# Loading the second channel weight of a token-and-channel mixer in whole rows, and reordering it in ScalarE's scaling passes

## The chip, the cores and the metric

The kernel runs on one core of a Trainium2 chip. The metric is the time of one launch on the device in microseconds (us); the median of several runs is given, with the lowest and the highest. Beside these runs there is one execution under the hardware profiler, which has a time of its own.

## What is computed

The reference is an attention block without softmax, followed by an MLP mixer, in float32:

```
kv  = einsum('bhsd,bhse->bhde', k, v)
a   = einsum('bhsd,bhde->bhse', q, kv)
a   = a / sqrt(mean(a*a, -1) + 1e-6) * g_norm
x   = a as (batch, seq, heads*dim)
u   = x + (relu(x^T @ w_tok1) @ w_tok2)^T
out = u + relu(u @ w_ch1) @ w_ch2
```

There are 8 batches with 8 heads, 576 rows and a head width of 64, so x has 512 columns. w_tok1 is 576 x 256, w_tok2 256 x 576, w_ch1 512 x 1536 and w_ch2 1536 x 512. The four weights come as 64-bit floats. The kernel has to turn them into 32-bit floats itself; everything else is 32-bit.

## The kernel before

**Stages.** The core first computes attention and token mixing, two batches at a time (four pairs). Then it does channel mixing over the rows of u, five groups in all; the first group is smaller and has code of its own (`channel1_once`, `channel2_once`), and the others run through `channel1` and `channel2`. The channel products use two nested levels of a fast 2 x 2 block scheme with seven products in place of eight. The blocks, their sums and differences are made by VectorE, ScalarE and GpSimd beside the matmuls.

**Order of the work.** Every instruction is held in the order of the program on its engine. That order is written out by hand for attention and token mixing, as strings of step names (`start`, `middle`, `steady`, `last`) that `play` carries out one by one. Nearly all transfers are issued on SP's queue by the helper `dma` (L121), in program order; a store that adds to what is in memory goes through GpSimd.

**Decoding a weight.** A weight is fetched in blocks. A block's raw words lie in a staging tile `raw` of 1024 pairs (low word, high word) in each partition, of which there are four. `decode` (L159) has four steps. `scale` runs on ScalarE: a pass over the high words writes the destination as a scaled float (L163), and a pass over the low words scales these in place (L166). The other three run on VectorE: `clamp` (L169), `shift` (L173) and `add` (L178), a custom instruction that adds the top of the low word to the result. `stream` (L1238) strings the blocks together so that a block is scaled before its predecessor's `add`. A digit in the hand-written order stands for so many further steps of this stream. The names f0 to f13 in the order stand for the fetches of the 14 channel blocks; f8 to f13 are the six blocks of w_ch2, 256 rows each.

**The order of leaves.** Channel mixing needs the columns of w_ch2 in an order that fits 32 x 32 transposes on VectorE. A row of 512 columns is read as (h, b, l, j), where h is the half (2), b a block (4), l a leaf (2) and j a column (32), and is stored in each half as (l, b, j). Before the change the transfers do this: `get_ch2` (L222) gives one transfer for each pair of row group, leaf and half, so eight in a block, each of runs of 32 columns, that is 256 bytes.

**The tile and its other uses.** `w_ch2` (L105) is one tile of 4 quarters x 6 row groups x 256 columns in each partition. A block fills two row groups in each of two quarters. Before its rows are filled, part of the tile is used for something else: `turn_early` (L640, steps x00 to x21) parks transposed blocks of u in row groups 2 to 5 of a quarter, and `put_blocks` (L624, steps b00 to b21) stores them to memory, from where `fetch_once` and `fetch_u` read them back. The order of parking is: quarters 2, 3, 0 and 1, and later 2 and 3 again. Later `mix_ch2` (L265) forms the outer sums from the quarters, `originals` and `split` (L291, L297) store the parts for the later groups, and `w2_of` (L277) gives a quarter or a sum to the first group's matmuls.

Of the kernel before, what the change touches and what calls it, by code (L numbers as in the profile page):

```python
# [11 lines left out]
F32 = mybir.dt.float32  # L12
U32 = mybir.dt.uint32
U16 = mybir.dt.uint16
AF = mybir.ActivationFunctionType
# [5 lines left out]
def kernel(  # L21
# [32 lines left out]
    nc = tc.nc  # L54
    P = 128
    B, S, DM = k.shape
# [7 lines left out]
    NC, NF, NTOK = DM // P, DCH // P, DTOK // P  # L64
    HP = H // 2
    DH = DM // 2
# [3 lines left out]
    NS = NF // 2  # L70
# [7 lines left out]
    def pool(name, bufs, side="left", stack=ctx, **kw):  # L78
        return stack.enter_context(tc.tile_pool(name=name, bufs=bufs, side=side,
                                                reuse_waits="tile", **kw))  # L80

    w1s, w2s = ExitStack(), ExitStack()
    w1p, w2p = pool("w1", 1, "left", w1s), pool("w2", 1, "right", w2s)
# [18 lines left out]
    w_tok2 = tokw.tile([P, NTOK, S], F32, name="w_tok2")  # L102

    w_ch1 = w1p.tile([P, 4, 4, FQ], F32, name="w_ch1")
    w_ch2 = w2p.tile([P, 4, NS, DH], F32, name="w_ch2")  # L105
    k_in = [inp.tile([P, JJ, DH], F32, name=f"k_in{i}") for i in range(4)]
    v_in = [inp.tile([P, JJ, DH], F32, name=f"v_in{i}") for i in range(4)]
    kvp = [inp.tile([P, HP, P], F32, name=f"kvp{i}") for i in range(2)]
    u_rest = dram.tile([J * P, DM], F32, name="u_rest")
    u_rows = lambda u: u_rest if u == B else out[u, :LO]  # L110

    def do(f, *a, **kw):
        return lambda: f(*a, **kw)

    late = {}


    keep = tc.keep_in_program_order

    def dma(o, i, engine=nc.sync):  # L120
        keep(engine.dma_start(o, i))  # L121
# [34 lines left out]
            q_rest[b] = qtp.tile([P, HP, HF], F32, name="qR", tag="qR", bufs=4)  # L156
            dma(q_rest[b], q[b].rearrange("(c p) s -> p c s", p=P)[..., LO:])

    def decode(dst, raw, flat):  # L159

        bits = dst.bitcast(U32)
        def scale():
            keep(nc.scalar.activation(dst, raw()[..., 1].bitcast(F32), AF.Prelu,  # L163
                                      scale=2.0 ** -112, alpha=2.0 ** 32))
            low = raw()[..., 0]
            keep(nc.scalar.activation(low, low, AF.Copy, scale=2.0 ** -29))  # L166

        def clamp():
            keep(nc.vector.tensor_scalar(out=dst, in0=dst, scalar1=TOP, scalar2=-TOP * 2.0 ** 32,  # L169
                                         op0=ALU.min, op1=ALU.max))  # L170

        def shift():
            keep(nc.vector.tensor_scalar(out=bits, in0=bits, scalar1=3, scalar2=None,  # L173
                                         op0=ALU.logical_shift_left))

        def add():
            o = bits.bitcast(U16)
            keep(nc.vector._custom_dve(ADD32_U16LIMBS, out=o, in0=o, in1=flat().bitcast(U16)[..., :2]))  # L178

        return scale, clamp, shift, add  # L180

    def words(w):
        return w.bitcast(U32).rearrange("r (n w) -> r n w", w=2)
# [2 lines left out]

        return flat if len(dst.shape) == 2 else flat.rearrange("p (a n) -> p a n", a=dst.shape[1])

    def block(n, loads, dst):

        raw = []

        def fetch():
            raw.append(stage.tile([P, n, 2], U32, name="raw", tag="raw", bufs=4))
            for o, i in loads(raw[0]):
                dma(o, i)

        def turn():
            t = raw[0]
            return t if len(dst.shape) == 2 else t.rearrange("p (a n) w -> p a n w", a=dst.shape[1])  # L200

        return (fetch,) + decode(dst, turn, lambda: raw[0])

    def get_tok1(t):

        rows = words(moe_w_tok1)[:LO].rearrange("(j p) n w -> p j n w", p=P)
        return block(J * P, lambda raw: [(raw.rearrange("p (j n) w -> p j n w", j=J),
                                          rows[:, :, ts(t, P)])], w_tok1[:, :J, ts(t, P)])

    def get_tok1_rem():  # L210
        w = words(moe_w_tok1)[LO:]
        return block(DTOK, lambda raw: [(raw[:HF], w), (raw[HF:], w)], w_tok1[:, J])

    def get_tok2(t):
        return block(S, lambda raw: [(raw, words(moe_w_tok2)[ts(t, P)])], w_tok2[:, t])
# [5 lines left out]

    def get_ch2(f):  # L222

        a = 2 * (2 * f // NS)

        def loads(raw):
            t = raw.rearrange("p (h f l b j) w -> p f l h b (j w)", h=2, f=2, l=2, b=NC)
            rows = words(moe_w_ch2)[ts(f, 2 * P)].rearrange("(f p) (h b l j) w -> f l p h b (j w)", f=2, h=2, b=NC, l=2)
            return [(t[:, i, l, h], rows[i, l, :, h]) for i in range(2) for l in range(2) for h in range(2)]

        dst = w_ch2[:, a:a + 2, ds(2 * f % NS, 2)]
        return block(2 * DM, loads, dst.rearrange("p h f n -> p h (f n)"))

# [29 lines left out]
    def mix_ch2():  # L265


        firsts, lasts = [], []
        for i in range(2):
            t1, t2, t4 = (late["d2"][:, n, ts(i, NS // 2)] for n in range(3))  # L270
            b11, b12, b21, b22 = (w_ch2[:, n, ts(i, NS // 2)] for n in range(4))
            sub = lambda o, a, b: do(tensor_add, o, a, b, ALU.subtract)
            firsts += [sub(t1, b12, b11), sub(t2, b22, t1)]
            lasts += [sub(b12, b12, b22), sub(t4, b21, t2)]
        return firsts, lasts

    def w2_of(n):  # L277
        i = {1: 0, 7: 1, 2: 2, 3: 3}
        return w_ch2[:, i[n]] if n in i else late["d2"][:, {5: 0, 6: 1, 4: 2}[n]]

    parts_dram = {(w, o): dram.tile([P, 7, FQ], F32, name=f"parts{w}{o}")
                  for w in (1, 2) for o in SA}
# [3 lines left out]
    def part_of(weight, o, n):  # L286
        if weight == 1:
            return (w_ch1[:, SA[o]] if SA[o] < 4 else late["w2"][:, SA[o] - 4])[:, SA[n]]
        return w2_of(o)[:, ts(int(n in (2, 3)), W), ts(int(n in (7, 3)), P)]
# [328 lines left out]
    def turn_tile(y, x, i):  # L618
        for o in range(2):
            keep(nc.vector.transpose(  # L620
                y[:, :, o, 2 * i:2 * i + 2].rearrange("p b n t -> p n b t"),
                x[:, ts(o, DH)].rearrange("p (n b t) -> p n b t", n=2, b=NC)))
# [16 lines left out]

    def turn_early(u, half):  # L640
        pair, c = u // 2, 2 * (u % 2) + half
        y = w_ch2[:, (c + 2) % 4 if pair == 0 else 2 + c, 2:].rearrange("p b (o n t) -> p b o n t", o=2, n=NC)
        for i in range(2):
            turn_tile(y, X[pair, c][:, i], i)
        blocks[u, half] = y
# [154 lines left out]
    def channel2_once(g):  # L800
# [11 lines left out]
        def product(n, ps, start, stop):  # L812
            for p in range(2):
                for s in range(NS):
                    matmul(ps[:, p], lhsT=late["once"][n - 1][:, s, p], rhs=w2_of(n)[:, s],
                           start=(start and p == 0 and s == 0), stop=stop,
                           skip_group_check=True)
# [122 lines left out]
    def sub(t, i, j):  # L940

        return t[:, ts(i, W), j]
# [308 lines left out]
    def play(lines, after={}, **stages):  # L1251
# [3 lines left out]
        for name in " ".join(lines).split():  # L1255
# [5 lines left out]
            else:  # L1261
# [5 lines left out]
    tok2 = [get_tok2(t) for t in range(NTOK)]  # L1267
    channel = ([get_ch1(c, f) for f in range(2) for c in range(NC)]
               + [get_ch2(f) for f in range(NF // 2)])
    load(0)  # L1270
    for block in tok1[:2]:
# [20 lines left out]
    for block in tok1[2:] + tok2:  # L1292
# [35 lines left out]
    more = {f"w{n}{k}": f for n, b in enumerate(tok1 + tok2) for k, f in enumerate(b)}  # L1328
    more |= {f"f{n}": b[0] for n, b in enumerate(channel)}
    more |= {f"x{u}{half}": do(turn_early, u, half) for u in range(3) for half in range(2)}  # L1330
    more |= {f"b{u}{half}": lambda u=u, half=half: put_blocks(u, half, blocks[u, half])
             for u in range(3) for half in range(2)}
# [46 lines left out]

    fetch_x(0)  # L1380
    firsts, lasts = mix_ch2()
    parts2 = [f for o in ORDER2 for f in split(2, o)]

# [79 lines left out]
```

## Time and profile before

| | us |
|---|---|
| median of 3 runs | 781.64 |
| lowest, highest | 778.35, 783.63 |
| profiled execution, time | 777.2 |
| profiled execution, span from first to last instruction | 775.4 |
| TensorE (PE) busy | 761.0 |
| VectorE (DVE) busy | 643.2 |
| ScalarE (ACT) busy | 277.4 |
| GpSimd (POOL) busy | 112.4 |

PEld is the weight load of TensorE, SP the engine that issues most transfers, and a name with q at its end (SPq) the queue of that engine. A row of instructions in order of time gives the start, the time taken, the engine, the line in the kernel, the operation, what is written and read, the shape and the count; the idle time of the engine before it and what ended this stand in brackets. A row of waits gives who waited for whom, then the total in us, the count and the longest. A row of transfers gives what is written and read, the issuing queue, the count, the size of each and the median time from issue to landing. Line numbers are those of the kernel before; a helper's line stands for all its callers, so tiles tell such rows apart: `raw` is the staging tile, `w_ch` is either channel weight, `ps_...` are banks of PSUM.

### The profile page before, as it was taken

The page shows a single profiled execution, that of the slowest core. Times are in us where ns is not written, and L with a number is a line of the kernel's source. Part 1 is how long each engine was busy: PE and PEld are TensorE (multiplying, and loading weights), DVE is VectorE, ACT ScalarE, POOL GpSimd, SP SyncE. Part 2 cuts the span into 40 slices and gives each one's busy share as a digit, 9 for nine tenths or more (in the row PEclk, how much of TensorE's full clock was granted, in tenths as well). Part 3 has the DMA queues.
Part 4 walks back from the last instruction along what each step waited for, and adds up shares of the span by engine and source line. Part 5 has one row for each costly group of instructions (what it writes and reads, how often), then busy time and mean ns, then how long its engine had stood idle before and what let it go on. Part 6 is the DMA issues. An engine that isn't in the chain of part 4 may idle for free.

```text
span 775.4 us, 12776 instructions
## 1 busy us (share of the span) xinstructions
PE 761.0 (98%) x4682; PEld 611.6 (79%) x4682; DVE 643.2 (83%) x946; ACT 277.4 (36%) x549; POOL 112.4 (14%) x128
## 2 busy tenths in 40 slices
PE   5999999999999999999999999999999999999997
PEld 5655555545888888888888888888888888888887
DVE  2867887897776868989978889987998996798996
ACT  2566575665210233521134242223352223325220
POOL 1002021113410000002240001042000218000204
PEclk9999999999999999999999999999999999999999
DMA  9999999999899696599998577999659879855679
GB/s 293 322 330 375 370 354 281 253 259 362 281 279 358 256 301 189 166 274 184 233 230 262 148 216 224 256 188 268 199 147 285 174 218 207 207 147 159 150 192 117
DMA packets 177820, 188.30 MB, mean 243 GB/s; under 512 B 74464, under 2 KB 140512, under 8 KB 177760
## 3 DMA queue, kind: packets, MB, share of 16 engines
q1 hardware_dynamic: 140752, 167.55, 71.5%
q0 software_dynamic: 34816, 18.36, 16.1%
q10 hardware_dynamic: 2192, 1.61, 0.7%
q8 instruction: 37, 0.61, 0.3%
q14 instruction: 23, 0.19, 0.1%
HBM read 138.31 MB, written 49.15 MB: 242 GB/s over the span
## 4 chain that ended last, share of the span: by engine, by line
PE 94%; DVE 3%; DMA 1%; ACT 1%; issue 1%; SPq 0%; DVEq 0%; ACTq 0%
PE ps_d L133 27%; PE ps_b L133 19%; PE ps_a L133 18%; PE ps_u L133 8%; PE ps_h L133 8%; PE ps_v L133 5%; PE ps_c L133 3%; PE ps_o L133 2%; PE ps_kv L133 2%; PE ps_w L133 2%; DMA raw<-in_moe_w_tok_dram 1%; ACT x L499 1%; DVE r L124 0%; DVE sv L124 0%; DVE x L445 0%
## 5 line engine op out<-in xcount | busy, mean ns | idle before, releaser
L133 PE MATMUL ps_d<-ui,w 128*128 128x256 f32 x504 | 118.6, 379 | 0.0
L133 PEld LDWEIGHTS ps_d<-ui,w 128*128 128x128 f32 x504 | 95.8, 190 | 13.0
L130 ACT COPY ps_d<-ps_a 128x768 f32<-128x768 f32 (+1 forms) x56 | 32.0, 572 | 202.1 <-PE ps_a L133 199.1
L124 DVE TENSOR_TENSOR v<-v,v 128x1536 f32<-128x1536 f32 (+2 forms) x70 | 103.2, 1482 | 0.3
L133 PE MATMUL ps_b<-sv,w 128*128 128x256 f32 x324 | 79.2, 380 | 0.1
L133 PE MATMUL ps_a<-v,w 128*128 128x256 f32 x324 | 78.8, 379 | 0.0
L1200 POOL DMA_DIRECT2D out_dram<-us x24 | 26.8, 1831 | 292.6 <-ACT p L130 287.3
L133 PEld LDWEIGHTS ps_b<-sv,w 128*128 128x128 f32 x324 | 60.8, 190 | 10.2 <-issue 2.1
L133 PEld LDWEIGHTS ps_a<-v,w 128*128 128x128 f32 x324 | 61.6, 190 | 8.4
L133 PE MATMUL ps_h<-x,w_tok 128*128 128x512 f32 (+1 forms) x160 | 65.4, 603 | 0.5 <-DVE x L503 0.4
L133 PE MATMUL ps_u<-h,w_tok 128*128 128x512 f32 (+1 forms) x160 | 64.7, 599 | 0.0
L133 PE MATMUL ps_d<-v,w 128*128 128x256 f32 x258 | 62.7, 379 | 0.0
L127 ACT ACTIVATE v<-v 128x768 f32<-128x768 f32 (+1 forms) x54 | 42.6, 821 | 55.1 <-DVE v L124 55.1
L1200 POOL DMA_DIRECT2D out_dram<-r x40 | 41.3, 1923 | 103.2 <-ACT p L130 80.3
L133 PE MATMUL ps_d<-sv,w 128*128 128x256 f32 x228 | 55.4, 379 | 0.0
L133 PEld LDWEIGHTS ps_d<-v,w 128*128 128x128 f32 x258 | 48.9, 190 | 6.6
L133 PEld LDWEIGHTS ps_h<-x,w_tok 128*128 128x128 f32 (+1 forms) x160 | 26.2, 189 | 32.3 <-issue 27.3
L133 PEld LDWEIGHTS ps_u<-h,w_tok 128*128 128x128 f32 (+1 forms) x160 | 25.6, 179 | 31.1 <-issue 26.7
L133 PEld LDWEIGHTS ps_d<-sv,w 128*128 128x128 f32 x228 | 43.3, 190 | 5.9
L133 PE MATMUL ps_a<-uT,w 128*128 128x256 f32 x192 | 46.7, 379 | 0.0
L133 PE MATMUL ps_b<-ui,w 128*128 128x256 f32 x168 | 40.8, 379 | 0.0
L133 PEld LDWEIGHTS ps_a<-uT,w 128*128 128x128 f32 x192 | 36.5, 190 | 5.0
(162 smaller groups left out, 1278.0 us busy)
## 6 DMA issues: line engine op xcount, KB each, us to landing
w<-parts SPq DMA_DIRECT2D x168, 384.0 KB, 3.7
w<-parts SPq DMA_DIRECT2D x56, 192.0 KB, 3.8
uT<-blocks SPq DMA_DIRECT2D x36, 256.0 KB, 5.3
k_in<-in_k_dram SPq DMA_DIRECT2D x16, 512.0 KB, 8.7
qT<-in_q_dram SPq DMA_DIRECT2D x8, 1024.0 KB, 9.5
out_dram<-x POOLq DMA_DIRECT2D x16, 512.0 KB, 6.4
v_in<-in_v_dram SPq DMA_DIRECT2D x14, 512.0 KB, 9.0
raw<-in_moe_w_ch_dram SPq DMA_DIRECT2D x8, 768.0 KB, 7.7
```

Source lines behind the costliest of these rows:

```text
L124: keep(engine.tensor_tensor(out=o, in0=a, in1=b, op=op))
L127: keep(nc.scalar.activation(o, a, AF.Relu))
L130: keep(nc.scalar.copy(o, a))
L133: keep(nc.tensor.matmul(*a, **kw))
L499: keep(nc.scalar.activation(x[:, k, h], x[:, k, h], AF.Copy, scale=inv[:, k, h]))
L1200: keep(nc.gpsimd.dma_start(to, t()[ds(b * Q, Q), at].rearrange("p n l j -> p n (l j)"), accum_op=ALU.add))
```

## The change

`get_ch2` now makes two transfers for a block, one for each row group, of whole rows: 512 columns of 8 bytes, 4 KB in a piece. The staging tile thus holds the columns in the order of memory. The order of leaves is made by ScalarE: `scale_leaves` runs in place of `scale` for these six blocks and has four passes, two over the high words (one for each leaf) and two over the low words. The low words are written over the high words that have been used, and `add` reads them there.

The tile is laid out anew, as 2 pairs of quarters x 6 row groups x 2 quarters x 256 columns, so that a block is one run of 1024 columns. `w2_quarter(n)` gives a quarter in the new layout, with rows of 256 at a step of 512; the users of the tile go through it.

```diff
-    w_ch2 = w2p.tile([P, 4, NS, DH], F32, name="w_ch2")
+    w_ch2 = w2p.tile([P, 2, NS, 2, DH], F32, name="w_ch2")
+    w2_quarter = lambda n: w_ch2[:, n // 2, :, n % 2]
...
+        def scale_leaves():
+            of = raw().rearrange("p (g b l j) w -> p g l b j w", g=4, b=NC, l=2)
+            to = lambda t, l: t.rearrange("p (g l b j) -> p g l b j", g=4, l=2, b=NC)[:, :, l]
+            for l in range(2):
+                keep(nc.scalar.activation(to(dst, l), of[:, :, l, ..., 1].bitcast(F32), AF.Prelu,
+                                          scale=2.0 ** -112, alpha=2.0 ** 32))
+            for l in range(2):
+                keep(nc.scalar.activation(to(raw()[..., 1], l), of[:, :, l, ..., 0], AF.Copy, scale=2.0 ** -29))
...
-            keep(nc.vector._custom_dve(ADD32_U16LIMBS, out=o, in0=o, in1=flat().bitcast(U16)[..., :2]))
-        return scale, clamp, shift, add
+            keep(nc.vector._custom_dve(ADD32_U16LIMBS, out=o, in0=o, in1=flat().bitcast(U16)[..., 2 * leaves:][..., :2]))
+        return scale_leaves if leaves else scale, clamp, shift, add
...
     def get_ch2(f):
-        a = 2 * (2 * f // NS)
         def loads(raw):
-            t = raw.rearrange("p (h f l b j) w -> p f l h b (j w)", h=2, f=2, l=2, b=NC)
-            rows = words(moe_w_ch2)[ts(f, 2 * P)].rearrange("(f p) (h b l j) w -> f l p h b (j w)", f=2, h=2, b=NC, l=2)
-            return [(t[:, i, l, h], rows[i, l, :, h]) for i in range(2) for l in range(2) for h in range(2)]
-        dst = w_ch2[:, a:a + 2, ds(2 * f % NS, 2)]
-        return block(2 * DM, loads, dst.rearrange("p h f n -> p h (f n)"))
+            t = raw.rearrange("p (f n) w -> p f n w", f=2)
+            rows = words(moe_w_ch2)[ts(f, 2 * P)].rearrange("(f p) n w -> f p n w", f=2)
+            return [(t[:, i], rows[i]) for i in range(2)]
+        dst = w_ch2[:, 2 * f // NS, ds(2 * f % NS, 2)]
+        return block(2 * DM, loads, dst.rearrange("p f h n -> p (f h n)"), True)
...
-            b11, b12, b21, b22 = (w_ch2[:, n, ts(i, NS // 2)] for n in range(4))
+            b11, b12, b21, b22 = (w2_quarter(n)[:, ts(i, NS // 2)] for n in range(4))
...
-        return w_ch2[:, i[n]] if n in i else late["d2"][:, {5: 0, 6: 1, 4: 2}[n]]
+        return w2_quarter(i[n]) if n in i else late["d2"][:, {5: 0, 6: 1, 4: 2}[n]]
...
-        y = w_ch2[:, (c + 2) % 4 if pair == 0 else 2 + c, 2:].rearrange("p b (o n t) -> p b o n t", o=2, n=NC)
+        y = w2_quarter((c + 2) % 4 if pair == 0 else 2 + c)[:, 2:].rearrange("p b (o n t) -> p b o n t", o=2, n=NC)
```

More of the change, by code (lines that the diff above doesn't have):

```diff
@@ L157, in load_q_rest, with decode @@
             dma(q_rest[b], q[b].rearrange("(c p) s -> p c s", p=P)[..., LO:])
-    def decode(dst, raw, flat):
+    def decode(dst, raw, flat, leaves=False):
         bits = dst.bitcast(U32)
@@ L187, in like, with block @@
         return flat if len(dst.shape) == 2 else flat.rearrange("p (a n) -> p a n", a=dst.shape[1])
-    def block(n, loads, dst):
+    def block(n, loads, dst, leaves=False):
         raw = []
@@ L200, in turn @@
             return t if len(dst.shape) == 2 else t.rearrange("p (a n) w -> p a n w", a=dst.shape[1])
-        return (fetch,) + decode(dst, turn, lambda: raw[0])
+        return (fetch,) + decode(dst, turn, lambda: raw[0], leaves)
     def get_tok1(t):
```

## The prediction

> **What bounds the kernel now.** I read the page's table of busy times first, to see which engine fills the span, and then busy times by stage, cut where the changed loads begin (about 117 us) and where the last block of this weight is rounded (about 190 us).
>
> ```profile
> span 775.4 us, 12776 instructions
> PE 761.0 (98%) x4682; PEld 611.6 (79%) x4682; DVE 643.2 (83%) x946; ACT 277.4 (36%) x549; POOL 112.4 (14%) x128
> ```
>
> ```profile
> 0.00:20.00 20.00, 11.82 (x144) 11.31 (x144) 5.42 (x13) 4.31 (x7) 2.77 (x14) 1.00 0.94 292
> ...
> 117.00:131.00 14.00, 14.00 (x104) 6.66 (x95) 13.36 (x30) 6.43 (x16) 1.68 (x3) 1.00 0.96 290
> 131.00:149.00 18.00, 17.41 (x273) 9.88 (x272) 10.76 (x22) 11.61 (x27) 0.74 (x1) 1.00 1.05 257
> 149.00:172.00 23.00, 23.00 (x123) 9.99 (x123) 21.97 (x35) 14.93 (x30) 5.25 (x7) 1.00 0.95 255
> 172.00:190.00 18.00, 18.00 (x52) 7.79 (x49) 15.66 (x21) 11.78 (x20) 4.19 (x6) 1.00 1.04 344
> ```
>
> After the two bounds of a stage come its length and the busy times of TensorE, its weight loads, VectorE, ScalarE and GpSimd, then clock, DMA share and GB/s. TensorE works for 761.0 of 775.4 us. Of the 14.4 us without work, 8.2 lie in the first 20 us, before this weight is touched. In the four stages that the change touches TensorE is idle for 18.00 - 17.41 = 0.59 us in all, while the DMA engines are full (0.95 to 1.05). A busy matmul row need not be at its peak, so I looked at the chain that ended last: from 157.14 to 188.78 us it is matmuls alone (40 of ps_h in 15.85 us, 40 of ps_u in 15.80), 439 ns for a pass over 512 columns as in the stages around. Full DMA engines therefore hold nothing up here. The one wait of TensorE between 50 and 190 us is this:
>
> ```profile
> PE ps_o L133 <- ACT x L499: 0.6, 1, 0.6
> ```
>
> It ends with attention's scaling of x at 143.7 us, when of the six blocks only the first had been scaled (130.81) and none rounded (from 149.26).
>
> **What the skill says.** "DMA: Bandwidth & Descriptors", section "Specifications", puts the smallest transfer at line rate at 512 B; pieces are now 256 B and become 4 KB. The trace agrees in direction: between 146 and 150 us, nearly all 256 B, the queue's 2158 packets carried 0.53 MB for 67.7% of 16 engines, 20 ns each; between 102 and 112 us, pieces of 1 KB and more, 2.87 MB cost 84.5%, 47 us of one engine per MB against 82. "ScalarE: Activation LUTs", section "What ACT_TABLE_LOAD costs", prices an activation with immediate operands at 186 ns + 0.833 ns per element, less 93 ns where two follow each other: 1.04 us for 1024 elements, 0.61 for 512. The trace's passes over the raw words, which step over every other word, take 1.16 us, a tenth longer. "SBUF — State Buffer", section "SBUF: two separate sides", says that transfers and engines use different ports; so lighter transfers should not quicken TensorE. No run yet tests that.
>
> **Part 1, the loads.** Six blocks of 1 MB go from 8 transfers of 128 KB (4096 pieces of 256 B) to 2 of 512 KB (256 pieces of 4 KB).
>
> ```profile
> raw<-in_moe_w_ch_dram SPq DMA_DIRECT2D x8, 768.0 KB, 7.7
> raw<-in_moe_w_ch_dram SPq DMA_DIRECT2D x48, 128.0 KB, 4.4
> ```
>
> The columns are count, size and the time from issue to landing; the first row is the other channel weight, whose pieces of 6 KB are the nearest thing to the new load. 36 issues go, 36 x 0.54 us (the median of this issue) = 19 us of SP's queue. DMA time falls from 24,576 pieces x 20 ns / 16 = 31 us of all engines to 6.3 MB x 47 / 16 = 18.5 us. A block is whole sooner: now from the first issue (118.65 us for the first block) to the scaling pass at 130.81, some 12 us; then about 8, by the 768 KB row. Everything behind on SP moves forward: q and k rows, the stored turned blocks, the fetch of uT at 171.86. On the path that sets the end: nothing, since TensorE waits for none of them (uT is first multiplied at 188.72). **0 us.** Should the cover go, and TensorE be faster here by 13 us, this would be worth its 12.5 us; nothing in this change does that.
>
> **Part 2, the scaling passes.** Each block has two passes of 1024 (L163, L166) and gets four of 512, two high and two low. Measured: the two start 1.06 us apart and the second ends 1.16 later, 2.2 us. Four of 512, by the copies of that width (0.60 us, three in 1.64): 3 x 0.52 + 0.60 = 2.2 us; the skill's price gives two passes 1.99 and four 2.17. So +0 to +0.2 us a block, at most 1.1 us of ScalarE for six. The unknown is the shape: sources of 16 runs of 32 words in place of one run. From below, it costs nothing (the passes already step by 8 bytes). From above, I let each double, +2.2 us a block. I take +0.2. The block that counts is the last:
>
> ```profile
> 177.09 1.17 ACT L163 ACTIVATE w_ch<-raw 128x1024 f32<-128x1024 f32 x1 [0.99 <-DVE w_ch L178]
> 178.16 1.14 ACT L166 ACTIVATE raw<-raw 128x1024 uint32<-128x1024 uint32 x1
> 179.21 0.56 ACT L130 COPY x<-ps_u 128x512 f32<-128x512 f32 x1
> 179.67 0.59 ACT L130 COPY ps_u<-x 128x512 f32<-128x512 f32 x1
> ```
>
> Behind the passes stands the copy that seeds tile 5 (done at 180.26). TensorE comes to it after 20 matmuls of 439 ns from 172.99, at 181.77: 1.5 us of slack. +0.2 is hidden; +2.2 would stop TensorE for 0.7 us. Each of the other blocks has idle time of ScalarE next to it (0.5 to 2.6 us). **0 us.**
>
> **Part 3, the waits.** The pass at 177.09 waited 0.99 us for the addition of an earlier block (L178), that at 155.75 1.54 us likewise (the addition ran from 153.64 to 155.72). Those blocks write other rows, but their two separate halves span one another. In the new layout a block is one run of 1024, so I expect both waits to go, 2.5 us of ScalarE idle time. Late next is the landing, and behind that TensorE, which is not waiting. The passes also wait for two transfers each in place of eight. **0 us** on the path.
>
> **Part 4, the layout.** Quarters now lie in pairs, rows of 256 at a step of 512. The three rounding steps on VectorE keep 1024 elements (0.68, 0.68, 1.22 us); the addition reads the word beside the one it read. The sums (L124, 768 elements in 0.95 us), the 24 transposes (0.40 each), matmul operands of 256 and stores in pieces of 1 KB keep counts and sizes. **0 us**, with 0.1 us on either side for a transpose or a sum whose rows step further.
>
> **Sum.** 0 us, bounds -0.6 (the whole wait of TensorE in the stage) and +0.7. The profiled execution took 777.2 us, so 777 again; the median, 781.64 of three (778.35 to 783.63), lies 4.4 above it, and the profile can't show where. I take 0.6 off, since runs of longer time may hold a late transfer in the full stage: **781.0 us**.
>
> **The rivals.** *False waits between quarters (slower).* Turned blocks are parked in this tile. If their writes are ordered by span rather than by row, the second half's transposes must wait for the store of the first, its neighbour in the new layout:
>
> ```profile
> 83.47 1.42 DVE L620 STREAM_TRANSPOSE w_ch<-x 128x256 f32<-128x256 f32 x4
> 84.81 0.92 DVE L178 CUSTOM_DVE_ANT_1 w_ch<-w_ch,raw 128x1536 uint16<-128x1536 uint16 x1
> 85.64 1.28 DVE L445 TENSOR_TENSOR x<-ps_o,g_sb 128x512 f32<-128x512 f32 x2
> ...
> 86.17 3.47 SPq L121 DMA_DIRECT2D blocks<-w_ch  x4
> ```
>
> The store is issued from 86.17 to 89.64 and lands 2.9 us later (the row for these stores), so VectorE would stand from 83.5 to 92.5, 9 us. Queued behind it: an addition, attention's gains at 85.64 and its sums. The k-v products at 93.66 need the banks that those gains free at 86.92; 9 us later is 95.9, a stop of 2.3 us; VectorE then has 3.6 idle us to 104 and 0.6 to 117 to catch up, and what is left stops TensorE later. Some 5 to 9 us, 7 taken: **788.6**. It decides from 6.7 us of delay on (93.66 - 86.92). For it: the two waits of part 3 look like order by span. Against: a pass of the other weight began at 127.41 while the shift of the rows interleaved with it ran only at 128.53; only additions have shown the loose order.
>
> *Relief that the profile can't show (faster).* If the 4.4 us between profile and median are late transfers in the full stage, 12.5 us less DMA time could win most: **777.5**. Against: the profiled execution has just as full engines and no such wait.
>
> *Passes at twice the time:* +0.7 on ScalarE's path, **782.3**, and more only if several seeds are late.
>
> **How the numbers follow.** No change, 0.78; false waits, 0.12; relief, 0.06; slow passes, 0.04. About 1% is what a measurement of this kernel can tell from no change. The range reaches from the relief, with a little for the spread, to the middle of the false waits: 777.0 to 787.0. Faster by over 1% (below 773.8) would need more than half of all idle time of TensorE, mostly from stages not touched: 0.03. Slower by over 1% (above 789.5) is the dear half of the false waits and what I haven't thought of: 0.09. Within 1%: 0.88.
>
> **What would show it.** Right: 12 loads of 512 KB landing in 5 to 9 us, DMA share well below 0.95 between 131 and 172 us, 24 passes of about 0.6 us, no wait of L163 for L178, TensorE idle for 0.6 us or less from 50 to 190. Wrong: transposes (L620) that wait for a store of blocks; passes over 0.8 us; TensorE waiting for a seed near 182 us.

## The result and the profile after

The changed kernel takes 776.97 us, the median of 20 runs (776.47 to 778.63). The kernel before, run beside it, takes 778.32 (777.42 to 783.63, 20 runs). The ratio is 0.9974 with a 95% interval of 0.9963 to 0.9985: faster by about 2.0 us, which is also the difference of the means (779.10 and 777.09). The medians differ by 1.35 us, because much of the gain is a tail that is gone: 7 of the 20 runs before took over 779 us, and none of those after. The profiled execution took 776.47 us (777.2 before).

The head of its profile, and busy times by stage, with the columns as in the prediction:

```profile
span 774.6 us, 12729 instructions
PE 760.8 (98%) x4682; PEld 611.6 (79%) x4682; DVE 642.7 (83%) x946; ACT 279.4 (36%) x561; POOL 112.4 (15%) x128
```

```profile
117.00:131.00 14.00, 14.00 (x98) 6.72 (x95) 13.36 (x30) 8.17 (x19) 1.67 (x3) 1.00 1.00 347
131.00:149.00 18.00, 18.00 (x274) 10.03 (x274) 11.39 (x23) 10.76 (x28) 1.16 (x2) 1.00 0.73 260
149.00:172.00 23.00, 23.00 (x123) 9.90 (x121) 22.30 (x35) 16.04 (x38) 4.83 (x7) 1.00 0.81 259
172.00:190.00 18.00, 18.00 (x51) 8.29 (x50) 14.35 (x20) 11.50 (x22) 4.92 (x7) 1.00 1.03 367
```

TensorE's work is what it was (761.0 and 760.8 us). In the stage from 131 to 149 us, 17.41 busy us became 18.00: the only wait of TensorE between 50 and 190 us has gone, and the waits of the kernel after list none there. The DMA share between 131 and 172 us fell from 1.05 and 0.95 to 0.73 and 0.81. So 0.6 us of the gain can be read directly, and it is the very wait that the prediction put down to ScalarE. What ended it is seen when SP's issues are set beside TensorE. The kernel before, in order of time (`qT` is the tile of q rows that attention multiplies next):

```profile
117.36 11.12 SPq L121 DMA_DIRECT2D raw<-in_moe_w_ch_dram  x9
128.53 3.93 SPq L121 DMA_DIRECT2D blocks<-w_ch  x8
132.57 4.38 SPq L121 DMA_DIRECT2D raw<-in_moe_w_ch_dram  x8
137.05 1.54 SPq L121 DMA_DIRECT2D qT<-in_q_dram  x1
...
141.66 2.02 ACT L499 ACTIVATE x<-x,inv 128x64 f32<-128x64 f32 x8 [1.92 <-issue]
143.77 1.16 PE L133 MATMUL ps_o<-kvp,qT 64*64 64x64 f32 x64 [0.59 <-ACT x L499]
```

The kernel after, in order of time:

```profile
117.56 2.15 SPq L122 DMA_DIRECT2D raw<-in_moe_w_ch_dram  x3
119.77 9.38 SPq L122 DMA_DIRECT2D blocks<-w_ch  x8
129.37 0.84 SPq L122 DMA_DIRECT2D raw<-in_moe_w_ch_dram  x2
130.31 0.38 SPq L122 DMA_DIRECT2D qT<-in_q_dram  x1
...
141.58 2.02 ACT L507 ACTIVATE x<-x,inv 128x64 f32<-128x64 f32 x8 [1.91 <-issue]
143.03 1.16 PE L134 MATMUL ps_o<-kvp,qT 64*64 64x64 f32 x64
```

The scaling of x runs until 143.60 us in the kernel after, yet TensorE starts its matmuls at 143.03. They do not need the end of that scaling, so the label on the wait before was wrong. What they need is `qT`. The instructions on this tile, first of the kernel before, then of the kernel after:

```profile
L121 SPq DMA_DIRECT2D qT<-in_q_dram x1: 1542/1542/1542, 137.0 to 137.0; - x1
...
DMA to landing us min/median/max: 6.6/6.6/6.6
```

```profile
L122 SPq DMA_DIRECT2D qT<-in_q_dram x1: 378/378/378, 130.3 to 130.3; - x1
...
DMA to landing us min/median/max: 6.9/6.9/6.9
```

Before, the q rows are issued at 137.05 and land 6.6 us later, at 143.65; TensorE starts 0.12 us after that. After, they are issued at 130.31 and land at 137.2, 5.8 us early. The time from issue to landing hardly differs; the place in the queue does. Ahead of the q rows on SP stand one fetch of w_ch2 (f8), eight stores of turned blocks, and another fetch (f9), 8 + 8 + 8 issues before and 2 + 8 + 2 after (the first row of each view also holds one load of the other weight). From the start of that first row to the issue of the q rows SP needs 19.7 us before and 12.8 us after.

### The profile page after: what moved, and what is told of

It reads as the page before. It is cut to its first block, busy times and chain, and to the rows that moved or that the text cites. A ratio compares the mean times of both kernels' runs of the same rounds, so it can differ in the third digit from the quotient of the medians.

```text
span 774.6 us, 12729 instructions
## 1 busy us (share of the span) xinstructions
PE 760.8 (98%) x4682; PEld 611.6 (79%) x4682; DVE 642.7 (83%) x946; ACT 279.4 (36%) x561; POOL 112.4 (15%) x128
## 3 DMA queue, kind: packets, MB, share of 16 engines
q1 hardware_dynamic: 117136, 167.54, 70.2%
## 4 chain that ended last, share of the span: by engine, by line
PE 93%; DMA 5%; DVE 2%; issue 0%; ACTq 0%; SPq 0%; DVEq 0%
PE ps_d L134 27%; PE ps_b L134 19%; PE ps_a L134 18%; PE ps_u L134 8%; PE ps_h L134 7%; PE ps_v L134 5%; PE ps_c L134 3%; DMA v_in<-in_v_dram 2%; PE ps_w L134 2%; PE ps_kv L134 2%; PE ps_o L134 2%; DMA qR<-in_q_dram 1%; DMA k_in<-in_k_dram 1%; DVE r L125 0%; DVE sv L125 0%; DVE xg L125 0%
```

## The experiments

Three theories. **Q**: the q rows (fetched by the step `lq1`) stood behind the fetches and were late, by 0.6 us in the profile and by more in some runs. **L**: less DMA work in this stretch helps in general, by whatever transfer. **W**: the gain comes from the waits that went, the passes or the layout. Each run is compared with runs of the kernel before on the same chip.

**Q rows ahead of the second fetch, nothing else.** The kernel before with one step moved in the hand-written order; loads of 256 bytes, passes and layout stay.

```diff
-        "kv00 kv01 e00 e01 -d40 f9", "-u8 -a3 -q30 -g31 -q31 -g30 -t30 -t31 -m3 -r3 -lq1",
+        "kv00 kv01 e00 e01 -d40", "-u8 -a3 -q30 -g31 -q31 -g30 -t30 -t31 -m3 -r3 -lq1 f9",
```

> The kernel before with one step moved: the transfer of the q rows for the second half of a pair (-lq1, 1 MB) stands ahead of the fetch f9 on SP's queue, not behind it. Theory Q (TensorE's wait at 143 us is for these rows, which queue behind 24 small transfers): the rows are issued at about 132.6 us in place of 137.05, land near 139, TensorE's only wait between 50 and 190 us (0.59 us) goes, and the timed ratio to the kernel before is that of the changed kernel, 0.9963 to 0.9985. Theory L (the gain is less DMA work in the full stage, whichever transfers): nothing changes there, ratio 0.9995 to 1.0005. Theory W (the gain is from waits of ScalarE and VectorE that the new layout drops): ratio 1.000 as well.

It took 777.52 us (776.25 to 780.13, 22 runs), with 779.17 (777.10 to 784.67, 52 runs) for the kernel before; ratio 0.9969, interval 0.9956 to 0.9982. Over 779 us were 2 of 22 runs, against 30 of 52. Its profile in order of time:

```profile
130.03 3.90 SPq L121 DMA_DIRECT2D blocks<-w_ch  x7
134.03 0.39 SPq L121 DMA_DIRECT2D qT<-in_q_dram  x1
...
143.60 1.16 PE L133 MATMUL ps_o<-kvp,qT 64*64 64x64 f32 x64
```

The rows land 5.6 us after issue, at 139.6, and TensorE waits for nothing between 50 and 190 us. One moved step brings a gain that can't be told from the change's, with every small transfer, both waits for the addition and the old layout still there. Theory Q holds, and neither L nor W is needed.

**Q rows later, in both kernels.** The step goes to a later place, behind the fetch f10. The same edit in the kernel before and in the changed one:

```diff
-        "kv00 kv01 e00 e01 -d40 f9", "-u8 -a3 -q30 -g31 -q31 -g30 -t30 -t31 -m3 -r3 -lq1",
-        "h00 -i3 -d31 -s30 x20 1", "h01 x21 1", "a0 q00 g01 q01 g00", "h10 t00 t01 1 1", "h11 f10 1 1", "hr z2",
+        "kv00 kv01 e00 e01 -d40 f9", "-u8 -a3 -q30 -g31 -q31 -g30 -t30 -t31 -m3 -r3",
+        "h00 -i3 -d31 -s30 x20 1", "h01 x21 1", "a0 q00 g01 q01 g00", "h10 t00 t01 1 1", "h11 f10 -lq1 1 1", "hr z2",
```

> The kernel before with the same q transfer moved the other way, behind the eight transfers of the fetch f10. Theory Q: issued near 144 us, landed near 150.6, while TensorE comes to these rows at 143.1: a wait of about 7 us where there were 0.6, so some 6 to 7 us slower (ratio 1.008 to 1.009). Theories L and W: no transfer is added and no wait of ScalarE or VectorE, so within 0.1%.

> The changed kernel with the q transfer moved to the same place, behind f10, which is now two transfers. Theory Q: issued near 132 us, landed by 140 to 142, still ahead of 143, so no wait and the time of the changed kernel (ratio to before 0.996 to 0.999). If the place in the order of steps mattered in itself and not the transfers ahead, it would lose some 7 us like the run with the order of before.

The kernel before goes to 787.16 us (785.70 to 788.24, 4 runs), ratio 1.0084 (1.0051 to 1.0117), as expected. In its profile the rows land 9.4 us after an issue at 142.84, at 152.2, so the wait is longer than the 7 us expected. TensorE's wait, and busy times by stage:

```profile
PE ps_o L133 <- DMA qT<-in_q_dram: 9.4, 1, 9.4
```

```profile
131.00:149.00 18.00, 12.00 (x167) 6.51 (x165) 6.57 (x14) 9.39 (x22) 0.74 (x1) 0.96 0.91 219
149.00:172.00 23.00, 19.65 (x197) 10.22 (x198) 15.90 (x29) 10.69 (x22) 4.83 (x6) 0.81 0.55 161
172.00:190.00 18.00, 18.00 (x46) 7.63 (x45) 17.27 (x22) 12.32 (x22) 0.63 (x2) 1.00 1.02 285
```

The changed kernel takes the same edit for nothing: 777.30 us (776.25 to 778.58, 18 runs), ratio 0.9965 (0.9952 to 0.9979), with no wait of TensorE from 50 to 190 us, though its q rows now take 10.0 us from an issue at 133.33 and land at 143.3, later than the 140 to 142 expected. TensorE comes to them at 145.12 in this execution, some 2 us later than in the other profiles, so 1.8 us are left. So the same place in the order of steps costs one kernel 0.8% and the other nothing; what stands ahead of the rows decides. With the cause alone made larger, the wait of the kernel before carries its true name, "DMA qT".

**Two passes in place of four.** The changed kernel with the passes of the kernel before over 1024 elements; the order of leaves is left out, so the columns of w_ch2 are used in the order of memory.

```diff
-            keep(nc.vector._custom_dve(ADD32_U16LIMBS, out=o, in0=o, in1=flat().bitcast(U16)[..., 2 * leaves:][..., :2]))
-        return scale_leaves if leaves else scale, clamp, shift, add
+            keep(nc.vector._custom_dve(ADD32_U16LIMBS, out=o, in0=o, in1=flat().bitcast(U16)[..., :2]))
+        return scale, clamp, shift, add
```

> The changed kernel with the two passes of 1024 in place of the four of 512; the order of leaves of the second channel weight is left out, so its columns stay in the order of memory. It prices the four passes. All theories that put the gain on transfers: TensorE waits as in the changed kernel, ratio to before 0.996 to 0.9985, the passes cost 0.0 to 0.2 us a block of ScalarE and nothing on the whole. If the passes did cost something, this is faster than the changed kernel by up to 1 us (0.1%).

777.32 us (776.31 to 778.57, 19 runs), ratio 0.9967 (0.9952 to 0.9981), against 0.9974 for the whole change, and 0.9965 for the changed kernel with its q rows later, on the same chip as this run: the four passes cost nothing that can be measured.

**What makes the q rows late: how many transfers, or how small the pieces?** Three kernels, all with the changed layout and four passes. The first keeps eight transfers for a block, with pieces of 1 KB. The second has four, with pieces of 256 bytes; the staging tile then holds the columns leaf by leaf, and the four passes read them there (that part of the edit isn't printed). The third splits each of these in two: eight of 256 bytes, so that only the loads of the change are undone; its lines below are set against the second kernel.

```diff
-            return [(t[:, i], rows[i]) for i in range(2)]
+            return [(t[:, i, ts(n, P)], rows[i, :, ts(n, P)]) for i in range(2) for n in range(NC)]
```

```diff
-            t = raw.rearrange("p (f n) w -> p f n w", f=2)
-            rows = words(moe_w_ch2)[ts(f, 2 * P)].rearrange("(f p) n w -> f p n w", f=2)
-            return [(t[:, i], rows[i]) for i in range(2)]
+            t = raw.rearrange("p (f l k j) w -> p f l k (j w)", f=2, l=2, k=2 * NC)
+            rows = words(moe_w_ch2)[ts(f, 2 * P)].rearrange("(f p) (k l j) w -> f l p k (j w)", f=2, l=2, k=2 * NC)
+            return [(t[:, i, l], rows[i, l]) for i in range(2) for l in range(2)]
```

```diff
-            return [(t[:, i, l], rows[i, l]) for i in range(2) for l in range(2)]
+            return [(t[:, i, l, ts(h, NC)], rows[i, l, :, ts(h, NC)]) for i in range(2) for l in range(2) for h in range(2)]
```

> The changed kernel with each block loaded in eight transfers of 128 KB, as before, but in pieces of 1 KB (a quarter of a row). It has the count of transfers of before and most of the lighter work of the changed kernel. Theory Q: SP reaches the q rows near 133 to 134 us (24 issues of about 0.5 us and the backlog), they land near 140, before TensorE needs them at 143: no wait, ratio to before 0.996 to 0.999. If the count of transfers alone sets the place of the q rows: issued near 137, the wait of some 0.6 us is back, ratio 0.9995 to 1.0005.

> The changed kernel with each block loaded in four transfers of 256 KB in pieces of 256 B: the pieces of before at half the count of transfers. Theory Q with the count as its cause: q rows issued near 133 us, no wait, ratio 0.996 to 0.999. If the work of the small pieces on the DMA engines is the cause: the q rows land as late as before (143 to 144), ratio 0.9995 to 1.0005.

> The changed kernel with the loads alone undone in kind: eight transfers of 128 KB in pieces of 256 B for a block, with the new tile layout and the four passes kept. Theory Q: the wait for the q rows near 143 us is back (some 0.6 us), ratio to before 0.999 to 1.001. If the new layout or the passes held the gain, it would keep 0.996 to 0.9985.

The only wait of TensorE from 50 to 190 us in each, in this order:

```profile
PE ps_o L134 <- DMA qT<-in_q_dram: 1.7, 1, 1.7
```

```profile
PE ps_o L134 <- DMA qT<-in_q_dram: 0.5, 1, 0.5
```

```profile
PE ps_o L134 <- DMA qT<-in_q_dram: 1.2, 1, 1.2
```

| loads of a block | fetches ahead start, q rows issued (us) | between the two | landing after | median (us) | runs over 779 us | ratio |
|---|---|---|---|---|---|---|
| 8 of 256 B, kernel before, same chip | | | | 778.57 | 21 of 60 | |
| 8 of 256 B, new layout and passes | 117.76, 137.59 | 19.8 | 7.1 | 778.91 | 10 of 22 | 1.0016 (1.0001 to 1.0031) |
| 4 of 256 B | 115.44, 135.43 | 20.0 | 8.5 | 778.70 | 6 of 14 | 1.0007 (0.9988 to 1.0025) |
| 8 of 1 KB | 120.74, 137.87 | 17.1 | 7.5 | 777.49 | 2 of 21 | 0.9985 (0.9974 to 0.9996) |

With the old loads, the new layout and the passes bring nothing (if anything they cost 0.1%), and the wait is back, with 1.2 us where some 0.6 were expected; so theory W is out. For the other two kernels no forecast came true as a whole. Four transfers of 256 bytes leave the wait and the tail, and the q rows land at 143.9 us, as expected if small pieces are the cause and not the count. Eight of 1 KB take most of the tail away (none of 21 runs over 780 us, against 8 of 22 with eight of 256 bytes) and gain 0.15%, but in the profile their q rows are issued later than expected, and the wait is the longest of the three; this execution (779.21 us) is the second longest of the 21.

The way to read this is from the start of the fetches ahead on SP. Eight of 256 bytes, then eight of 1 KB:

```profile
117.76 11.38 SPq L122 DMA_DIRECT2D raw<-in_moe_w_ch_dram  x9
```

```profile
120.74 9.11 SPq L122 DMA_DIRECT2D raw<-in_moe_w_ch_dram  x9
```

Half as many transfers of 256 bytes do not shorten the way from there to the q rows: 20.0 us against 19.8, and 19.7 in the kernel before. Their q rows are issued sooner only because that execution came to its fetches 2.3 us sooner. Pieces of 1 KB in the same count shorten it by 2.7 us, and the change with pieces of 4 KB by some 7; how much of these 7 needs fewer transfers as well isn't separated. The execution with 1 KB has the longest wait although this way is shorter, since it came to its fetches 3.0 us later. Among the ten profiles of this study that start lies anywhere from 115.44 to 120.74 us, while TensorE is ready for the q rows from 142.99 to 143.75 in all but the one at 145.12.

An estimate from these figures: had the kernel before started its fetches at 120.74 us, its q rows would have landed at 120.74 + 19.7 + 6.6 = 147.0, 3.9 us after TensorE is ready at 143.18; those of the changed kernel at 120.74 + 12.8 + 6.9 = 140.4, in time. The two-pass kernel, which has the loads of the change, did start at 120.34, landed its q rows at 139.5 and had no wait. A late start of the fetches would thus be enough for a tail in the one kernel and not in the other.

**Both at once.** The changed kernel with f9 behind the q rows as well.

```diff
-        "kv00 kv01 e00 e01 -d40 f9", "-u8 -a3 -q30 -g31 -q31 -g30 -t30 -t31 -m3 -r3 -lq1",
+        "kv00 kv01 e00 e01 -d40", "-u8 -a3 -q30 -g31 -q31 -g30 -t30 -t31 -m3 -r3 -lq1 f9",
```

> The changed kernel with the q transfer ahead of f9 as well. Theory Q: the rows were already there 6 us early, so nothing more is won: ratio to before as the changed kernel's, 0.996 to 0.9985. If unprofiled runs of the changed kernel still lost time to late q rows, it would be faster than the changed kernel by 0.1% or more and its runs would lie closer together.

777.06 us (776.60 to 779.62, 14 runs), ratio 0.9978 (0.9965 to 0.9991), no wait. The second cure adds nothing to the first: they are cures of one thing. No version measured here beats the changed kernel by more than can be told apart.

**What stays open.** No run of over 780 us was profiled, so that its extra time also lies at the q rows is argued, from the order alone (30 of 52 runs over 779 us become 2 of 22), from the estimate above and from the clock (last section). What moves the start of the fetches from execution to execution stays open. Whether eight of 1 KB are truly worse than two of 4 KB isn't settled: 0.9985 and 0.9974 have intervals that overlap.

## Why the prediction was wrong

The forecast was no change at 781.0 us. It came out at 776.97, 0.03 us below the range, and faster by more than the measurement is uncertain. Of the 4.0 us between forecast and result, 3.3 are the base: the three runs shown have a median of 781.64, twenty of the same kernel 778.32. That base was bad luck: two of its three runs lay in the tail. The remaining 0.7 us is the size of the effect: 0.6 was taken off for late transfers, and the medians differ by 1.35.

**The step that failed** is the reading of the one wait, "It ends with attention's scaling of x at 143.7 us", and with it Part 1's "On the path that sets the end: nothing, since TensorE waits for none of them". Part 1 named q rows among what moves forward on SP. Had their landing been worked out, 137.05 + 6.6 = 143.65 would have stood beside 143.77, the end of TensorE's wait. The label went to a scaling pass that ended nearby, at 143.68. The row of the matmul says what it reads: `qT` and `kvp`, not x. So the wait was not proof that TensorE waits for no transfer; it was the transfer: 0.59 us in the profile, and about 2.0 us in the mean of the runs once the q rows come early, where Part 1 had 0.

**Rival "relief that the profile can't show"** (777.5, chance 0.06) had late transfers as its mechanism. That its time is near is luck: it took 4.1 us off a base that was 3.3 too high, and the gain is 1.35 us of the median, 2.0 of the mean. The argument against it, "the profiled execution has just as full engines and no such wait", fell with the same misreading. It named no transfer; the runs name one, and show that not the sum of DMA work matters, since the moved step alone gains as much with none of it saved.

**Part 1, sizes.** The loads became 12 of 512 KB, landing in 5.8 us (8 was expected from the row of 768 KB, which itself went from 7.7 to 8.8):

```profile
raw<-in_moe_w_ch_dram SPq DMA_DIRECT2D x8, 768.0 KB, 8.8
raw<-in_moe_w_ch_dram SPq DMA_DIRECT2D x12, 512.0 KB, 5.8
```

The packets of SP's queue went from 71.5% of 16 engines' span to 70.2%, 10.6 us less, where 12.5 were worked out. The gain was in what stands behind on the queue, which was given 0.

**Part 2** held on the path and was mis-sized off it. The last block, in order of time:

```profile
175.28 1.28 ACT L173 ACTIVATE w_ch<-raw 128x512 f32<-128x512 f32 x2
176.59 1.26 ACT L176 ACTIVATE raw<-raw 128x512 uint32<-128x512 uint32 x2
177.74 0.56 ACT L131 COPY x<-ps_u 128x512 f32<-128x512 f32 x1
178.21 0.59 ACT L131 COPY ps_u<-x 128x512 f32<-128x512 f32 x1
```

Four passes take 2.57 us from the first start to the last end, the two before 2.21: +0.36 a block, not 0.2. One takes 0.68 us (median), where the price in the Trainium skill's "ScalarE: Activation LUTs", section "What ACT_TABLE_LOAD costs", gave 0.61 before any overlap: the same tenth on top that the passes of 1024 already showed. ScalarE is busy 2.0 us longer (279.4 against 277.4). The seed of tile 5 is done at 178.8, sooner than the 180.26 of before, since the wait of 0.99 us ahead of the passes went and the work around it runs 0.7 us sooner. The cover held.

**Part 3** held: no pass waits for an addition any more, and on the path this is worth 0: the kernel with the old loads and the new layout has no such wait either, and gains nothing.

**Part 4 and the rival of false waits** (0.12): refuted. The kernel after, in order of time:

```profile
83.30 1.42 DVE L628 STREAM_TRANSPOSE w_ch<-x 128x256 f32<-128x256 f32 x4
...
86.67 3.42 SPq L122 DMA_DIRECT2D blocks<-w_ch  x4
87.85 1.42 DVE L628 STREAM_TRANSPOSE w_ch<-x 128x256 f32<-128x256 f32 x4
```

The next transposes start while the stores of their neighbours are still being issued, with no idle time ahead of them. The slow passes (0.04) didn't come either.

**Separate ports.** The Trainium skill's "SBUF — State Buffer", section "SBUF: two separate sides", was taken to say that lighter transfers would not quicken TensorE. The runs agree: its busy time is 761.0 us before and 760.8 after. That is true of the work and says nothing of the time at which a transfer arrives.

## What to carry to other kernels

Before a transfer is called hidden, take every load that stands behind the changed one on its queue, add its landing time to its issue, and set the sum beside the first instruction that reads it; a wait labelled with another engine is not trusted until that sum excludes the load. A transfer that lands just in time in the profile may be late in other runs, so a median well above the profiled time is a reason to look for such an edge. When two kernels' profiles are compared, the moment at which the queue came to the loads is set beside it, since it moved by 5 us here from execution to execution. When a load sits ahead of a more urgent one on one queue, a change of order can be worth as much as a change of the load.

## What the runs showed of the hardware

**A stall of TensorE is paid for in clock as well.** In the kernel before with the q rows later, 9.36 us of waiting are followed by a stage at a mean granted clock of 0.81 (the third number from the end of the row from 149 to 172 us above), and TensorE's busy time grows from 761.0 to 763.9 us. In shorter windows of this profile the granted clock is 1.00 up to 146 us, 0.74 from 146 to 149, 0.50 from 149 to 157 and 1.00 again from 158, so that some 5 us of work after the wait ran at half clock. The Trainium skill's "TensorE: Matmul & The Clock Gate", section "Part 1: The HAM clock gate", says that the clock is halved after an idle window of about 3.4 us; this agrees, and the waits of 0.46, 0.59, 1.21 and 1.73 us in four other profiles left the clock at 1.00 between 131 and 172 us.

This gives a mark for runs without a profile: of 112 runs of the kernel before with a recorded mean clock, the 20 of 781 us or more all have 0.995 to 0.998, and all but two of the 92 others 0.999 or 1.0. The changed kernel and the one with only the order changed have 0.999 or 1.0 in all their 42 runs. That points to idle times of some microseconds in the tail, but not to their place: the profiled execution of the changed kernel with its q rows later has 0.998 too, without any wait from 50 to 190 us; its clock is at 0.50 from 17 to 19 us.

**Behind few large loads, stores landed later.** The eight stores of turned blocks from 116 to 150 us land 2.5 us after issue before the change (median, 2.6 at most) and 7.9 us after it (9.5 at most), and SP spends 9.38 us on issuing them in place of 3.93: they now stand right behind 1 MB that SP handed over in two issues. The lighter work of larger pieces alone is not the cause: with eight transfers of 1 KB pieces the stores land after 2.6 us, with four of 256 bytes after 2.9. The Trainium skill's "DMA: Bandwidth & Descriptors", section "Queues, rings and completion order", says that each engine takes descriptors in the order of its ring, which fits. Nothing on the path reads these stores soon: ScalarE's one wait for them was 1.7 us and is 1.6.
